# The second slice of a two-stage MoE kernel and its sweep, reordered as one list of single steps

## The chip, the cores and the metric

The kernel runs on one core of a Trainium2 chip. The metric is the device time of one execution in microseconds. The median of three runs of the kernel before is 983.5 us (981.6 to 984.88).

## The reference

Attention over eightfold mean-pooled keys and values feeds a gated MoE block, and that a second block:

```python
x = attention(q, mean_pool8(k), mean_pool8(v))      # 4 x 8 heads, 576 x 64
x = x.reshape(2304, 512)                            # tokens x d_model
xn = x / sqrt(mean(x * x) + 1e-6) * rms_g           # first block
g, val = xn @ w_gate, xn @ w_val                    # d_ff = 1536
x = (g * sigmoid(g) * val) @ w_out
return ((x @ w_a) * (x @ w_b)) @ w_out2             # second block
```

## The kernel before

Every fp32 product is made of three TensorE matmuls on a high and a low part of each operand (`wl*xh`, `wh*xh`, `wh*xl`). ACT makes the high part by a cast (`ah`, `sh`, `rh`, `bh`, `woh`, `hh`, `xh_t`), and DVE or GpSimd (POOL) the low part by a subtraction (`al`, `sl`, `rl`, `bl`, `wol`, `hl`, `xl_t`). Each of them needs both the fp32 source and the high part, and TensorE needs both parts.

The first block's 2304 tokens go as tiles of 512 and 256, and as two slices of 768. A slice is cut into halves of 384 columns, and gate and value for one block f of 128 of the 1536 hidden features (12 blocks) are made with seven half-products instead of eight. These are the tokens `N<f>.1` to `.7` of the second slice (six matmuls of 384 columns each), `N<f+1>.6` being a product of block f that is put off. The other tokens of a block:

- `p1`, `p5`, `u2`: ACT copies of PSUM banks (L1295); `d1` to `d3`: DVE adds another bank (L1299); `z1`, `z2`: SiLU on ACT (L1303); `d4`, `d5`: the products gate x value (L1307, L1312), and their stores to DRAM as `h`.
- `e1` to `e4`: sums of weights (`sf`, L1326 to L1332), on DVE, or on POOL with a "!"; `ca`, `cs`, `cr`, `cb`: casts of weights on ACT (L1349); `la`, `ls`, `lr`, `lb`: their lows (L1355), on POOL, or on DVE with a "!".

A sweep follows each slice. It multiplies `h` with `w_out` and adds up 12 blocks in six banks, the tokens `U<f>.0` to `.5` in the second sweep: three matmuls of 512 columns in `.0` to `.3`, six of 256 in `.4` and `.5`; 72 adds in all (L1429). `U<f>.f` fetches weights (`wo_again`) and `h` (`hf`, a part of 512 columns and one of 256) by three DMAs; `.w` and `.x` make `woh` (ACT, L1400) and `wol` (L1403: POOL, or DVE with "!"); `.h0`, `.h1`, `.k0`, `.k1` make `hh` (ACT, L1413) and `hl` of both parts (L1416: DVE, or POOL with "!"). `Ue0` to `Ue5` evict the banks (`ev`, ACT, or DVE with "!") and store them. The first slice and its sweep have the same tokens with M and Q for N and U.

Four engines (TensorE, ACT, DVE, POOL) issue in the order in which the tokens are called, a list of words written out by hand; DMA issues on SP are ordered by the scheduler. Buffers are few: the three tiles `p1` hold the snapshot `p1`, the evictions `ev` and the 512-column part of `hf` in turn, two tiles `u2` the snapshot `u2` and the other part of `hf`, and each weight operand but `b` has two.

Before, the second slice's tokens form a regular pattern, the same for each f. The second sweep's list has a "+" behind each of its 72 adds; at these, the steps of `second_front` are spread evenly: four loads, the opening of a pool, the conversion of four weight blocks of the second block from the input's 64-bit words (ACT twice, DVE twice, POOL once each: L610, L611, L622, L634, L641), the loads of its x, its x forms (casts L845, lows L850, differences L854), and the weight operands of its f = 0 and 1 (`combine`: L939, L946, L961 to L967).

Of the kernel before, what the change touches and what calls it, by code (L numbers as in the profile page):

```python
# [85 lines left out]
N3.e1 N3.e2 N2.2 N2.p5 N3.la N3.e4 N3.cs N2.3 N2.d1 N2.z1 N3.ls N3.e3 N2.4 N2.u2 N3.cr N2.5 N2.d2
N2.z2 N3.lr N2.6 N1.d5 N2.cb N2.7 N2.d3 N2.d4 N2.lb N3.1 N3.p1 N4.ca N4.e1 N4.e2 N3.2 N3.p5 N4.la
N4.e4 N4.cs N3.3 N3.d1 N3.z1 N4.ls N4.e3 N3.4 N3.u2 N4.cr N3.5 N3.d2 N3.z2 N4.lr N3.6 N2.d5 N3.cb
N3.7 N3.d3 N3.d4 N3.lb N4.1 N4.p1 N5.ca N5.e1 N5.e2 N4.2 N4.p5 N5.la N5.e4 N5.cs N4.3 N4.d1 N4.z1
N5.ls N5.e3 N4.4 N4.u2 N5.cr N4.5 N4.d2 N4.z2 N5.lr N4.6 N3.d5 N4.cb N4.7 N4.d3 N4.d4 N4.lb N5.1  # L90
N5.p1 N6.ca N6.e1 N6.e2 N5.2 N5.p5 N6.la N6.e4 N6.cs N5.3 N5.d1 N5.z1 N6.ls N6.e3 N5.4 N5.u2 N6.cr
N5.5 N5.d2 N5.z2 N6.lr N5.6 N4.d5 N5.cb N5.7 N5.d3 N5.d4 N5.lb N6.1 N6.p1 N7.ca N7.e1 N7.e2 N6.2
N6.p5 N7.la N7.e4 N7.cs N6.3 N6.d1 N6.z1 N7.ls N7.e3 N6.4 N6.u2 N7.cr N6.5 N6.d2 N6.z2 N7.lr N6.6
N5.d5 N6.cb N6.7 N6.d3 N6.d4 N6.lb N7.1 N7.p1 N8.ca N8.e1 N8.e2 N7.2 N7.p5 N8.la N8.e4 N8.cs N7.3
N7.d1 N7.z1 N8.ls N8.e3 N7.4 N7.u2 N8.cr N7.5 N7.d2 N7.z2 N8.lr N7.6 N6.d5 N7.cb N7.7 N7.d3 N7.d4
N7.lb N8.1 N8.p1 N9.ca N9.e1 N9.e2 N8.2 N8.p5 N9.la N9.e4 N9.cs N8.3 N8.d1 N8.z1 N9.ls N9.e3 N8.4
N8.u2 N9.cr N8.5 N8.d2 N8.z2 N9.lr N8.6 N7.d5 N8.cb N8.7 N8.d3 N8.d4 N8.lb N9.1 N9.p1 N10.ca N10.e1
N10.e2 N9.2 N9.p5 N10.la N10.e4 N10.cs N9.3 N9.d1 N9.z1 N10.ls N10.e3 N9.4 N9.u2 N10.cr N9.5 N9.d2
N9.z2 N10.lr N9.6 N8.d5 N9.cb N9.7 N9.d3 N9.d4 N9.lb N10.1 N10.p1 N11.ca N11.e1 N11.e2 N10.2 N10.p5
N11.la N11.e4 N11.cs N10.3 N10.d1 N10.z1 N11.ls N11.e3 N10.4 N10.u2 N11.cr N10.5 N10.d2 N10.z2  # L100
N11.lr N10.6 N9.d5 N10.cb N10.7 N10.d3 N10.d4 N10.lb N11.1 N11.p1 N11.2 N11.p5 N11.3 N11.d1 N11.z1
U0.f N11.4 N11.u2 N11.5 N11.d2 N11.z2 U0.w U0.x U0.h0 N11.6 N10.d5 N11.cb U0.k0 U0.h1 N11.7 N11.d3
N11.d4 N11.lb U0.k1 U1.f
""".split()
SECOND_END = """
U0.0 + U1.w U0.1 + N12.6 N11.d5 U2.f U1.x U1.h0 U0.2 + U1.k0 U1.h1 U0.3 + U1.k1 U0.4 + U0.5 + U1.0
+ U3.f U2.w U1.1 + U2.x U2.h0 U1.2 + U2.k0 U2.h1 U1.3 + U2.k1 U1.4 + U1.5 + U2.0 + U4.f U3.w U2.1 +
U3.x U3.h0 U2.2 + U3.k0 U3.h1 U2.3 + U3.k1 U2.4 + U2.5 + U3.0 + U5.f U4.w U3.1 + U4.x U4.h0 U3.2 +
U4.k0 U4.h1 U3.3 + U4.k1 U3.4 + U3.5 + U4.0 + U6.f U5.w U4.1 + U5.x U5.h0 U4.2 + U5.k0 U5.h1 U4.3 +
U5.k1 U4.4 + U4.5 + U5.0 + U7.f U6.w U5.1 + U6.x U6.h0 U5.2 + U6.k0 U6.h1 U5.3 + U6.k1 U5.4 + U5.5  # L110
+ U6.0 + U8.f U7.w U6.1 + U7.x U7.h0 U6.2 + U7.k0 U7.h1 U6.3 + U7.k1 U6.4 + U6.5 + U7.0 + U9.f U8.w
U7.1 + U8.x U8.h0 U7.2 + U8.k0 U8.h1 U7.3 + U8.k1 U7.4 + U7.5 + U8.0 + U10.f U9.w U8.1 + U9.x U9.h0
U8.2 + U9.k0 U9.h1 U8.3 + U9.k1 U8.4 + U8.5 + U9.0 + U11.f U10.w U9.1 + U10.x U10.h0 U9.2 + U10.k0
U10.h1 U9.3 + U10.k1 U9.4 + U9.5 + U10.0 + U11.w U10.1 + U11.x U11.h0 U10.2 + U11.k0 U11.h1 U10.3 +
# [1445 lines left out]
```

## Time and profile before

| what | value |
|---|---|
| runs | 981.6, 983.5, 984.88 us |
| profiled execution | 982.69 us, span 981.0 us |
| granted TensorE clock | 0.993 of full speed, over the span |
| TensorE busy | 948.0 us (97%) |
| DVE, ACT, POOL busy | 620.9, 476.1, 339.7 us |

The span is the time from the first to the last instruction of the profiled execution; its device time is 1.69 us longer. Busy shares are of the span. A wait is put down to the instruction whose semaphore came last.

### The profile page before, as it was taken

The numbers are of one execution on the slowest core, as the hardware profiler recorded it, in microseconds if no ns is written. First come the engines' busy times: TensorE is split into PE (matmuls) and PEld (weight loads), VectorE is DVE, ScalarE is ACT, GpSimd is POOL, SyncE is SP. The second block draws the span as 40 slices with busy tenths as digits, with TensorE's granted clock in tenths as the row PEclk, the third lists the DMA queues.
The fourth block names the chain that finished last, engine by engine and source line by source line (L and its number), as shares of the span: only waits on it lengthen the run. The fifth ranks groups of instructions, "written<-read, shape, count | busy, mean of one in ns | idle before, by whom it ended". The sixth has DMA issues, their size and how long they took to land.

```text
span 981.0 us, 14651 instructions
## 1 busy us (share of the span) xinstructions
PE 948.0 (97%) x5194; PEld 860.2 (88%) x5194; DVE 620.9 (63%) x1070; ACT 476.1 (49%) x914; POOL 339.7 (35%) x326
## 2 busy tenths in 40 slices
...
GB/s 305 192 229 241 194 86 122 137 126 98 33 60 49 65 186 146 149 61 53 65 228 150 153 130 122 150 127 132 132 138 150 132 113 218 182 161 97 151 106 65
DMA packets 67945, 133.34 MB, mean 136 GB/s; under 512 B 7457, under 2 KB 31265, under 8 KB 67873
## 3 DMA queue, kind: packets, MB, share of 16 engines
...
q8 instruction: 41, 0.67, 0.3%
...
## 4 chain that ended last, share of the span: by engine, by line
PE 82%; DVE 5%; DMA 4%; ACT 3%; issue 2%; POOL 2%; SPq 1%; DVEq 0%; ACTq 0%; POOLq 0%
PE X L1029 24%; PE o L1132 15%; PE Y L1029 12%; PE o L1429 6%; PE Z L1029 6%; PE acc L691 6%; PE v L683 4%; PE g L683 4%; PE av L476 3%; PE sc L406 1%; POOL wol L1403 1%; DMA hf<-h 1%; PE eP L453 1%; PE xP L512 1%; DMA q<-in_q_dram 1%
## 5 line engine op out<-in xcount | busy, mean ns | idle before, releaser
L1110 DVE TENSOR_TENSOR hl<-hf,hh 128x768 fp32r<-128x768 f32 x36 | 35.5, 991 | 93.4 <-ACT hh L1109 93.4
L1132 PE MATMUL o<-woh,hl 128*128 128x512 f32 x216 | 85.8, 397 | 0.0
L1132 PE MATMUL o<-woh,hh 128*128 128x512 f32 x216 | 85.0, 394 | 0.0
L1132 PE MATMUL o<-wol,hh 128*128 128x512 f32 x216 | 84.7, 392 | 0.0
L1429 PE MATMUL o<-hh,wol 128*128 128x256 f32 (+1 forms) x192 | 67.5, 351 | 10.6 <-POOL wol L1403 10.6
L1109 ACT CAST hh<-hf 128x768 fp32r<-128x768 f32 x36 | 29.8, 834 | 87.0 <-PE o L1132 79.3
L1429 PE MATMUL o<-hh,woh 128*128 128x256 f32 (+1 forms) x192 | 66.6, 347 | 0.0
L1429 PE MATMUL o<-hl,woh 128*128 128x256 f32 (+1 forms) x192 | 66.5, 346 | 0.0
L641 POOL TENSOR_TENSOR w<-w,st 128x512 int32<-128x512 int32 x20 | 26.2, 1308 | 110.9 <-DVE w L634 70.8
L1037 ACT COPY p<-X 128x384 f32<-128x384 f32 x36 | 17.2, 478 | 89.7 <-PE X L1029 86.7
L673 POOL TENSOR_TENSOR wl<-wf,wh 128x512 fp32r<-128x512 f32 x27 | 35.7, 1330 | 68.2 <-ACT wh L669 68.2
L1429 PEld LDWEIGHTS o<-hh,wol 128*128 128x128 f32 x192 | 37.6, 196 | 15.8 <-POOL wol L1403 11.6
L1132 PEld LDWEIGHTS o<-woh,hh 128*128 128x128 f32 x216 | 40.5, 188 | 10.1
L1132 PEld LDWEIGHTS o<-wol,hh 128*128 128x128 f32 x216 | 40.6, 188 | 9.5
L1132 PEld LDWEIGHTS o<-woh,hl 128*128 128x128 f32 x216 | 40.6, 188 | 9.3
L611 ACT ACTIVATE st<-st 128x512 int32<-128x512 uint32 x72 | 48.0, 667 | 0.0
L1416 DVE TENSOR_TENSOR hl<-hf,hh 128x512 fp32r<-128x512 f32 (+1 forms) x37 | 30.3, 837 | 25.9 <-ACT hh L1413 25.9
L1029 PE MATMUL X<-xh_t,rl 128*128 128x384 f32 x120 | 41.0, 342 | 4.6 <-ACT u L1295 3.9
L641 POOL TENSOR_TENSOR wo<-wo,st 128x512 int32<-128x512 int32 x16 | 21.8, 1365 | 66.6 <-ACT p L1037 28.9
L691 PE MATMUL acc<-ht,wo 128*128 128x512 f32 (+1 forms) x112 | 43.5, 531 | 0.0
L1429 PEld LDWEIGHTS o<-hl,woh 128*128 128x128 f32 x192 | 37.4, 195 | 4.9 <-DVE hl L1416 0.6
L1029 PE MATMUL Y<-xh_b,rl 128*128 128x384 f32 x120 | 41.5, 346 | 0.2 <-ACT p L1037 0.2
(228 smaller groups left out, 3129.4 us busy)
## 6 DMA issues: line engine op xcount, KB each, us to landing
...
h<-p SPq DMA_DIRECT2D x60, 192.0 KB, 1.9
h<-u SPq DMA_DIRECT2D x60, 192.0 KB, 1.9
wo_again<-wd SPq DMA_DIRECT2D x36, 256.0 KB, 2.7
...
wd<-wo SPq DMA_DIRECT2D x24, 256.0 KB, 2.1
```

The lines of the kernel that those rows point to most:

```text
L476: nc.tensor.matmul(view[:, h0:h0 + len(hs), :D + 1], lhs, VB[b % 2][:, c, j0:j0 + len(hs), :], start=((c, bk) in ((0, 0), (2, 1))), stop=( ...
L611: nc.scalar.activation(out=low, in_=low.bitcast(U32), func=AF.Copy, scale=2.0 ** -29)
L641: (nc.vector if boot["alt"] else nc.gpsimd).tensor_tensor(out=bits, in0=bits, in1=low, op=ALU.add)
L673: (nc.vector if boot["alt"] else nc.gpsimd).tensor_sub(wl, wf[ph, f, i], wh.bitcast(F32))
L683: nc.tensor.matmul(bank[:, :n], w[:, c, :], x[:, c, cols], start=(c == 0 and i == 0), stop=(c == KD - 1 and i == 2),)
L691: nc.tensor.matmul(accs[c][:, cols], w[:, c, :], ht[:, :cols.stop - cols.start], start=(f == 0 and cols.start == 0), stop=(f == NF - 1),)
L1029: nc.tensor.matmul(dst[:, :HALF], w[:, c0 + c, :], x[:, c, :], start=(start and i == 0), stop=(stop and i == 5), skip_group_check=True,)
L1109: nc.scalar.copy(hh, hf)
L1110: nc.vector.tensor_sub(hl, hf, hh.bitcast(F32))
L1132: nc.tensor.matmul(accs[i], x[:, sub], y, start=(f == 0 and j == 0), stop=(f == NF - 1 and j == 2),)
L1416: (nc.gpsimd if boot["alt"] else nc.vector).tensor_sub(lo, src, hi.bitcast(F32))
L1429: nc.tensor.matmul(dst, w[:, c, :], x, start=(f == 0 and j == 0 and at == 0), stop=(f == NF - 1 and j == 2), skip_group_check=True,)
```

## The change

The second slice, its sweep and the second block's first operands are now one list. `second_front` no longer returns steps that are spread over the sweep; it registers a name for each: `Zo` (the pool), `ZL0`, `ZL1` (loads of x), `Z<form>c`, `Z<form>l` (cast and low of an x form), `Zd0` to `Zd3` (differences), `x0.0` to `x3.3` (four steps for each weight block's conversion), and `Z0.`, `Z1.` with `e1` to `e4`, `c` and `l` (weight operands). For each of them a "!" now chooses the engine. In the list, blocks x0 and x1 are converted wholly during the slice, x2 and x3 by half. The order within the slice and the sweep is no longer a repeated pattern, and many steps change engine: of the slice's 48 weight sums 30 are on POOL (4 before), of its 36 lows `la`, `ls`, `lr` 28 are on DVE (6 before), of the sweep's 12 `wol` nine are on DVE (none before), and of the 24 `hl` seven are on POOL (none before). The end of the first sweep is rewritten too. Matmuls and their operands are the same.

```diff
-N0.3 Jt3l Qe5 N0.p5 N1.e4 N0.4 N0.u2 N1.e3! N0.7 N1.cr Jt4l N1.lr! N0.d3 N0.5 N0.d1 N0.z1 N0.d2
-N0.z2 N0.d4 N1.1 N1.p1 N2.ca N2.e1 N2.e2 N1.2 N1.p5 N2.la N2.e4 N2.cs N1.3 N1.d1 N1.z1 N2.ls N2.e3
...
+Qe0 N1.e2 Jt4c N0.lr! Qe1 Qe2 Q11.5 Q11.4 Jt3l N0.1 N1.e3! Qe3! N0.p1 l Jt4l N0.2 N0.4 N1.ca N1.cs
+N0.u2 N0.3 N0.p5 Qe4! Qe5! N1.la! N1.e4! N1.ls N0.7 N0.5 N2.ca N2.e1 N1.1 N0.d3 N1.6 N2.e2 N1.3
...
+N10.z1 N10.cb N10.7 N9.z2 N11.1 N10.d2 N10.z2 x1.3 N10.lb N10.d3 N11.6 N11.cr N11.p1 N10.d4 N9.d4
+N11.cb N11.2 N11.4 N11.p5 N11.u2 N11.lr! x3.1 N11.lb! N10.d5 N11.5 U0.f N11.7 N11.d2 U0.h1 N11.d3
...
-U11.k1 U10.4 + U10.5 + U11.0 Ue0 + U11.1 Ue1! + U11.2 Ue2 + U11.3 Ue3! + U11.4 Ue4 + U11.5 Ue5! +
...
+Z1.la! Zb10l U10.3 Zt2l Zt3l Zb11l Ue2 U11.3 U10.5 Z1.cr Z1.ls! U10.4 U11.k1 Z1.lr Ue3 U11.4 Zd3!
+Ue4! U11.5 Z1.lb! Zt4c Ue5! Zt4l
...
-        def pairs(steps, n):
-            out = [steps[i::n] for i in range(n)]
-            out, i = [], 0
-            for j in range(n):
-                k = -(-(len(steps) - i) // (n - j))
-                group_, i = steps[i:i + k], i + k
-                out.append(lambda g=group_: [st() for st in g])
-            return out
-
-        loads, steps = load_and_build(0, new, quarter)
-        first_ = pairs(convert(0, 0) + convert(0, 1) + combine(0), 8)
-        first_[3] = lambda st=first_[3]: (st(), loads[0]())
-        first_[7] = lambda st=first_[7]: (st(), loads[1]())
-        rest = convert(1, 0) + convert(1, 1) + combine(1)
-        return [load_part] * 4 + [open_pool] + first_ + pairs(steps + rest, 24)
+        part = {}
+        loads = load_x(0, quarter, part)
...
+
+        def cast(i):
+            hi, lo = XC[(1, 0), i] = new(0, i)
+            for c in range(2):
+                nc.scalar.copy(hi[:, c], part[FORM_OF[i]][c])
+
+        def low(i):
+            hi, lo = XC[(1, 0), i]
+            eng = nc.gpsimd if boot["alt"] else nc.vector
+            for c in range(2):
+                eng.tensor_sub(lo[:, c], part[FORM_OF[i]][c], hi[:, c].bitcast(F32))
+
+        def less(i):
+            dst, a, b = LESS[i]
+            eng = nc.gpsimd if boot["alt"] else nc.vector
+            for c in range(2):
+                eng.tensor_sub(part[dst][c], part[a][c], part[b][c])
...
+        names["Zo"] = open_pool
+        names["ZL0"], names["ZL1"] = loads
+        for i in FORM_OF:
+            names[f"Z{i}c"] = lambda i=i: cast(i)
+            names[f"Z{i}l"] = lambda i=i: low(i)
+        for i in range(4):
+            names[f"Zd{i}"] = lambda i=i: less(i)
+
+        def conversion(n):
+            box, (begin, sign, merge, end) = convert_steps(new_wf2)
+
+            def last():
+                end()
+                load_part()
+
+            for i, st in enumerate((begin, sign, merge, last)):
+                names[f"x{n}.{i}"] = st
+
+        for n in range(4):
+            conversion(n)
...
+        def sums(f, i):
+            if (f, i // 3) not in box:
+                box[f, i // 3] = wf_p.tile([P, KD, P], F32, tag="wf", name=f"sf_{f}_{i}")
+            t, s0 = box[f, i // 3], box.get((f, 0))
+            eng = nc.gpsimd if boot["alt"] else nc.vector
+            if i == 1:
+                eng.tensor_add(t[:, 0:2], w(f, 1, 0), w(f, 1, 1))
+            elif i == 2:
+                eng.tensor_sub(t[:, 2:4], t[:, 0:2], w(f, 0, 0))
+            elif i == 3:
+                eng.tensor_sub(t[:, 2:4], w(f, 0, 1), s0[:, 2:4])
+            else:
+                eng.tensor_sub(t[:, 0:2], w(f, 0, 0), w(f, 1, 0))
...
+        def part_cast(f, key):
+            src = source(f, key)
+            n = src.shape[1]
+            hi, lo = box[f, key] = [
+                two["e"].tile([P, n, P], F32R, tag=f"{key}{e}{f}", name=f"{key}{e}_1_{f}", bufs=1)
+                for e in "hl"
+            ]
+            nc.scalar.copy(hi, src)
+            for i, nm in enumerate({"a": (A00, A01), "s": (S1, S2), "r": (S3, S4), "b": (A11,)}[key]):
+                WC[(1, None, f), nm] = (hi, lo, 2 * i)
+
+        def part_low(f, key):
+            hi, lo = box[f, key]
+            (nc.vector if boot["alt"] else nc.gpsimd).tensor_sub(lo, source(f, key), hi.bitcast(F32))
+
+        for f in range(2):
+            for i in range(1, 5):
+                names[f"Z{f}.e{i}"] = lambda f=f, i=i: sums(f, i)
+            for key in "asrb":
+                names[f"Z{f}.c{key}"] = lambda f=f, key=key: part_cast(f, key)
+                names[f"Z{f}.l{key}"] = lambda f=f, key=key: part_low(f, key)
...
+        second_front()
         for t in SECOND:
             token(t)
-        side = second_front()
-        total = SECOND_END.count("+")
-        at = done = 0
-        for t in SECOND_END:
-            if t != "+":
-                token(t)
-                continue
-            at += 1
-            want = -(-len(side) * at // total)
-            while done < want:
-                side[done]()
-                done += 1
```

The start of the slice on ACT. `p_0` and `u_0` are the snapshots of block 0, `ev<-o_4` the eviction of the first sweep's bank 4, `rh`, `ah`, `sh` casts of weights, and `xh_t` the cast of an x form. Before:

```order
419 L1349 CAST ah_4223<-wf_0_1_313 128x512
420 L1295 COPY p_0_2_4226<-X_2_4216 128x384
421 L884 CAST xh_t_2_4228<-x_0_1_3208 128x768
422 L248 COPY ev<-o_4_3562 128x512
423 L248 COPY ev<-o_5_3661 128x512
424 L1295 COPY p_0_2_4256<-Y_2_4236 128x384
425 L1295 COPY u_0_2_4266<-X_2_4216 128x384
```

After the change:

```order
417 L249 COPY ev<-o_0_3635 128x512
418 L885 CAST xh_t_2_4191<-x_0_1_3208 128x768
419 L249 COPY ev<-o_1_3614 128x512
420 L249 COPY ev<-o_2_3585 128x512
421 L1368 COPY p_0_2_4226<-X_2_4214 128x384
422 L1422 CAST ah_4244<-wf_0_1_313 128x512
423 L1422 CAST sh_4247<-sf_4172 128x512
424 L1368 COPY u_0_2_4250<-X_2_4214 128x384
425 L1368 COPY p_0_2_4259<-Y_2_4231 128x384
```

The evictions of `o_4` and `o_5` (and `o_3`) have left ACT; those of `o_0` to `o_2` stand ahead of both snapshots, and two casts of weights between `p` and `u` where the second `xh_t` and two evictions stood.

The middle of the sweep. `wol_7` and its like are lows of the sweep's weights, `wf` conversion ends, `al_…`, `sl_0`, `rl` and `bl` lows of the second block's weights. POOL before:

```order
223 L641 TENSOR_TENSOR wf_1_0_5314<-wf_1_0_5314,st_0_0_5217 128x512
224 L641 TENSOR_TENSOR wf_1_0_5335<-wf_1_0_5335,st_0_1_5226 128x512
225 L1403 TENSOR_TENSOR wol_3_5348<-wo_again_5280,woh_3_5347 128x512
226 L946 TENSOR_TENSOR al_5373<-wf_1_0_5314,ah_5372 128x512
227 L946 TENSOR_TENSOR sl_5404<-sf_0_5375,sh_5403 128x512
228 L946 TENSOR_TENSOR rl_5408<-sf_0_5379,rh_5407 128x512
229 L1403 TENSOR_TENSOR wol_4_5420<-wo_again_5341,woh_4_5419 128x512
230 L946 TENSOR_TENSOR bl_5441<-wf_1_0_5335,bh_5440 128x256
231 L1403 TENSOR_TENSOR wol_5_5479<-wo_again_5413,woh_5_5478 128x512
232 L1403 TENSOR_TENSOR wol_6_5533<-wo_again_5472,woh_6_5532 128x512
233 L1403 TENSOR_TENSOR wol_7_5597<-wo_again_5526,woh_7_5596 128x512
```

DVE before, while POOL is at `wol_7`; `xl_b`, `xl_t` are lows of x forms, `x<-x,x` differences:

```order
655 L1416 TENSOR_TENSOR hl_6_5553<-hf_6_5476,hh_6_5552 128x256
656 L854 TENSOR_TENSOR x_0_0_0_5382<-x_1_1_0_5463,x_0_0_0_5382 128x384
657 L854 TENSOR_TENSOR x_0_0_1_5383<-x_1_1_1_5464,x_0_0_1_5383 128x384
658 L850 TENSOR_TENSOR xl_b_0_5559<-x_1_1_0_5463,xh_b_0_5558 128x384
659 L850 TENSOR_TENSOR xl_b_0_5559<-x_1_1_1_5464,xh_b_0_5558 128x384
660 L854 TENSOR_TENSOR x_1_0_0_5457<-x_1_1_0_5463,x_1_0_0_5457 128x384
661 L854 TENSOR_TENSOR x_1_0_1_5458<-x_1_1_1_5464,x_1_0_1_5458 128x384
662 L850 TENSOR_TENSOR xl_t_0_5585<-x_0_0_0_5382,xh_t_0_5584 128x384
663 L850 TENSOR_TENSOR xl_t_0_5585<-x_0_0_1_5383,xh_t_0_5584 128x384
664 L1416 TENSOR_TENSOR hl_7_5604<-hf_7_5528,hh_7_5603 128x512
```

DVE after the change, around the same `wol_7`; `sf` are weight sums of the second block, `hl_7` hidden lows:

```order
655 L1489 TENSOR_TENSOR hl_7_5575<-hf_7_5545,hh_7_5574 128x256
656 L1055 TENSOR_TENSOR sf_1_5606<-wf_1_1_4856 128x256
657 L1057 TENSOR_TENSOR sf_1_5606<-sf_1_5606,wf_1_1_4559 128x256
658 L1476 TENSOR_TENSOR wol_7_5584<-wo_again_5541,woh_7_5583 128x512
659 L1059 TENSOR_TENSOR sf_4_5475<-wf_1_0_4407,sf_1_5237 128x256
660 L1489 TENSOR_TENSOR hl_7_5595<-hf_7_5543,hh_7_5594 128x512
661 L1015 TENSOR_TENSOR xl_t_0_5565<-x_0_0_0_4901,xh_t_0_5564 128x384
662 L1015 TENSOR_TENSOR xl_t_0_5565<-x_0_0_1_4902,xh_t_0_5564 128x384
663 L1061 TENSOR_TENSOR sf_4_5658<-wf_1_1_4559,wf_1_1_4856 128x256
664 L1476 TENSOR_TENSOR wol_8_5651<-wo_again_5587,woh_8_5650 128x512
```

`wol_7` has moved from POOL's queue to DVE's, between two hidden lows; the run of differences and lows of x beside it is down to one form's low ahead of the next `wol`.

The end of the sweep on DVE. `hl_11` is the last hidden low of the sweep, in two parts, `ev` an eviction. Before:

```order
680 L1416 TENSOR_TENSOR hl_10_5759<-hf_10_5697,hh_10_5758 128x512
681 L1416 TENSOR_TENSOR hl_10_5769<-hf_10_5699,hh_10_5768 128x256
682 L961 TENSOR_TENSOR sf_1_5784<-wf_1_1_5731 128x256
683 L962 TENSOR_TENSOR sf_1_5784<-sf_1_5784,wf_1_1_5681 128x256
684 L966 TENSOR_TENSOR sf_1_5797<-wf_1_1_5681,sf_1_5784 128x256
685 L967 TENSOR_TENSOR sf_1_5797<-wf_1_1_5681,wf_1_1_5731 128x256
686 L1416 TENSOR_TENSOR hl_11_5808<-hf_11_5747,hh_11_5807 128x512
687 L1416 TENSOR_TENSOR hl_11_5818<-hf_11_5749,hh_11_5817 128x256
688 L246 COPY ev<-o_1_5222 128x512
```

After the change, first the run's head and then its tail; the rows between are lows of x forms:

```order
673 L1489 TENSOR_TENSOR hl_11_5780<-hf_11_5754,hh_11_5779 128x512
674 L1476 TENSOR_TENSOR wol_11_5787<-wo_again_5752,woh_11_5786 128x512
675 L1082 TENSOR_TENSOR rl_0_5687<-sf_4_5475,rh_0_5686 128x512
676 L1489 TENSOR_TENSOR hl_10_5773<-hf_10_5648,hh_10_5772 128x256
677 L1082 TENSOR_TENSOR sl_0_5707<-sf_1_5237,sh_0_5706 128x512
678 L1082 TENSOR_TENSOR al_1_5656<-wf_1_1_4559,ah_1_5655 128x512
679 L1015 TENSOR_TENSOR xl_b_0_5616<-x_0_1_0_4905,xh_b_0_5615 128x384
```

```order
685 L1015 TENSOR_TENSOR xl_b_0_5518<-x_1_1_0_5095,xh_b_0_5517 128x384
686 L1015 TENSOR_TENSOR xl_b_0_5518<-x_1_1_1_5096,xh_b_0_5517 128x384
687 L1082 TENSOR_TENSOR sl_1_5736<-sf_1_5606,sh_1_5735 128x512
688 L1489 TENSOR_TENSOR hl_11_5809<-hf_11_5756,hh_11_5808 128x256
689 L247 COPY ev<-o_4_5286 128x512
690 L1082 TENSOR_TENSOR bl_1_5799<-wf_1_1_4856,bh_1_5798 128x256
```

The weight sums have gone elsewhere. Weight lows `rl_0`, `sl_0`, `al_1`, `sl_1` and eight lows of x forms (`xl_b`, `xl_t`) now stand between `wol_11` and the last `hl_11`.

## Rows read from the trace of the kernel before

**Rows 1.** The page, part 1: busy time and share of the span, by engine.

```profile
PE 948.0 (97%) x5194; PEld 860.2 (88%) x5194; DVE 620.9 (63%) x1070; ACT 476.1 (49%) x914; POOL 339.7 (35%) x326
```

**Rows 2.** TensorE's waits, 398 to 558 us: total, times, longest.

```profile
PE o L1429 <- POOL wol L1403: 10.6, 4, 5.9
PE X L1029 <- ACT u L1295: 3.0, 1, 3.0
```

**Rows 3.** TensorE's timeline, its pauses in 404 to 541: start, length, what, idle before.

```profile
405.96 0.44 PE L1029 MATMUL X<-xh_t,rl 128*128 128x384 f32 x1 [2.96 <-ACT u L1295]
...
491.06 0.50 PE L1429 MATMUL o<-hh,wol 128*128 128x512 f32 x1 [1.04 <-POOL wol L1403]
...
508.25 0.50 PE L1429 MATMUL o<-hh,wol 128*128 128x512 f32 x1 [2.81 <-POOL wol L1403]
...
515.17 0.50 PE L1429 MATMUL o<-hh,wol 128*128 128x512 f32 x1 [0.88 <-POOL wol L1403]
...
533.88 0.80 PE L1429 MATMUL o<-hh,wol 128*128 128x512 f32 x1 [5.91 <-POOL wol L1403]
```

**Rows 4.** Windows of 5 us: busy by engine, PEclk granted clock, DMA share, GB/s.

```profile
510.00:515.00 5.00, 4.29 (x19) 3.41 (x18) 3.61 (x5) 3.46 (x8) 4.35 (x3) 0.73 0.84 252
515.00:520.00 5.00, 4.83 (x27) 4.25 (x28) 4.02 (x8) 2.77 (x7) 2.25 (x3) 1.00 0.62 187
535.00:540.00 5.00, 5.00 (x15) 4.03 (x14) 0.00 (x0) 0.00 (x0) 0.51 (x1) 0.50 0.00 0
```

**Rows 5.** The chain that ended last: start, length, what.

```profile
370.23 25.07 PE o L1429 x141
...
415.10 3.13 PE X L1029 x18
...
480.66 3.13 PE X L1029 x18
...
495.92 0.36 SPq L1089
...
526.01 7.82 POOL wol L1403
```

**Rows 6.** Windows by stretch: first slice, first sweep, four stretches of second slice and sweep.

```profile
239.17:342.48 103.31, 102.36 (x629) 101.27 (x629) 76.46 (x142) 68.49 (x136) 52.32 (x62) 1.00 0.16 55
350.68:395.30 44.62, 44.62 (x260) 39.22 (x260) 27.83 (x48) 22.58 (x44) 11.43 (x11) 1.00 0.51 153
398.66:415.10 16.44, 13.48 (x69) 13.16 (x68) 10.54 (x17) 8.38 (x18) 3.97 (x3) 0.90 0.53 177
415.10:480.66 65.56, 65.56 (x380) 65.56 (x379) 46.70 (x81) 39.34 (x82) 41.72 (x36) 1.00 0.16 57
491.06:533.88 42.82, 33.21 (x174) 28.05 (x174) 33.08 (x53) 22.57 (x48) 25.52 (x15) 0.95 0.67 208
533.88:557.70 23.82, 23.82 (x121) 20.69 (x122) 13.79 (x15) 8.62 (x17) 14.54 (x10) 0.87 0.26 86
```

**Rows 7.** DMA issues, 398 to 560: count, KB, median us to landing.

```profile
h<-u SPq DMA_DIRECT2D x12, 192.0 KB, 1.9
x<-ev SPq DMA_DIRECT2D x6, 256.0 KB, 2.5
hf<-h SPq DMA_DIRECT2D x12, 128.0 KB, 2.6
```

**Rows 8.** Groups by line and shape, 398 to 558: busy us, mean ns, idle before.

```profile
L1330 DVE TENSOR_TENSOR sf<-wf,sf 128x256 f32<-128x256 f32 x10 | 14.0, 1402 | 0.0
L1416 DVE TENSOR_TENSOR hl<-hf,hh 128x512 fp32r<-128x512 f32 x12 | 12.1, 1011 | 14.8 <-ACT hh L1413 14.8
L1328 DVE TENSOR_TENSOR sf<-sf,wf 128x256 f32<-128x256 f32 x11 | 4.7, 424 | 0.3
L1299 DVE TENSOR_TENSOR u<-u,Y 128x384 f32<-128x384 f32 x12 | 6.6, 554 | 4.5 <-PE Y L1029 2.4 <-issue 2.1
...
L1355 DVE TENSOR_TENSOR rl<-sf,rh 128x512 fp32r<-128x512 f32 x2 | 1.4, 686 | 3.1 <-ACT rh L1349 3.1
...
L1355 POOL TENSOR_TENSOR rl<-sf,rh 128x512 fp32r<-128x512 f32 x10 | 13.0, 1295 | 10.3 <-ACT rh L1349 9.2 <-issue 1.1
...
L1413 ACT CAST hh<-hf 128x512 fp32r<-128x512 f32 x12 | 7.4, 616 | 4.5 <-DMA hf<-h 4.5
```

More of the change, by code (lines that the diff above doesn't have):

```diff
@@ L86 @@
[L86 to L114, printed above, removed]
-U11.k1 U10.4 + U10.5 + U11.0 Ue0 + U11.1 Ue1! + U11.2 Ue2 + U11.3 Ue3! + U11.4 Ue4 + U11.5 Ue5! +
+Jb10c Q4.2 Q4.0 Q5.w Q5.k1! S17.9 Q4.3 Q6.h1 Q6.k1 Q5.k0! Q5.x! N0.e2! Q5.0 S16.11 S16.12 N0.e4
@@ new lines @@
+S17.10 Q5.5 N0.cb Q5.3 Q6.w Q5.2 Jb00l Q6.h0 Jb10l Q6.x! Q7.f Q5.4 N0.e3! Q6.4 Q6.5 Q6.k0 S17.11
+Q7.h1 Q5.1 Q8.f Q6.1 Q6.2 Q7.k1! S17.12 N0.lb Q9.f Q7.w Jb11c Jd0 Q7.x! Q6.3 Q6.0 Jd2 Q7.5 Q7.4
+Q7.h0 Q7.k0 Q8.h0 Jt1c Q7.3 Q8.w Q7.1 Q8.k0 Q8.x! Q8.h1 Q8.k1 Q7.2 Q9.h1 Q7.0 Q8.4 Q8.5 Jt1l Q9.k1
+Q9.w Q9.h0 Q8.3 Q8.0 Jd1 Q10.f Q9.x! Q8.1 Q8.2 Q11.f Jt2c Q9.k0 Q10.h1 Q10.h0 Q9.5 Q10.k1 Q9.2 Q9.0
+Jd3 Q10.w Q10.k0! Q9.4 Q9.3 Q9.1 Q10.x! Q10.2 Q11.h0 Jt2l Q10.3 Jb11l Q10.0 Q11.k0! Q11.h1 Q11.w
+Q11.x! Q10.1 N0.cs Q10.4 Q11.k1 Q10.5 Q11.1 N0.ca N0.ls! Q11.0 N1.e1! Q11.3 Jt3c N0.cr N0.la! Q11.2
```

46 lines of the change are left out of this document (37 added, 9 removed).

## The prediction

> **What bounds the kernel now.** I read the page first: TensorE (PE) is busy 948.0 of 981.0 us [rows 1]. All but 33 us is matmuls, and the change adds and removes none, so only PE's idle and slow time can move. Next I took PE's waits for the stretch that the diff rewrites, from the second slice's first matmul (398.66) to the second stage's first (557.70): 3.0 us behind ACT, once, and 10.6 us behind GpSimd's (POOL's) `wol`, four times [rows 2]. The timeline places them: 2.96 at the start of the slice, 1.04 where the sweep begins, and 2.81, 0.88 and 5.91 inside the sweep [rows 3], 13.6 us in all.
>
> Idle time is not the whole loss. In 5-us windows the granted clock is 0.73 after the stall of 2.81 and 0.50, the lower level of 1.2 GHz, after that of 5.91, but 1.00 after that of 0.88 [rows 4]. So I compare the stretch with the same work undisturbed. In the chain, one output block f of the slice repeats every (480.66 - 415.10)/9 = 7.284 us [rows 5]; 12 make 87.4. The sweep has 288 matmuls in 72 adds; in the first sweep 141 of the same mixture take 25.07 us [rows 5], so 288 take 51.2, or 0.71 an add. The floor is 138.6 us, the stretch takes 557.70 - 398.66 = 159.04 (its ends are the edges of the first and last of four windows [rows 6]), and **20.4 us** are to be had: 13.6 idle and 6.8 mostly half clock, some 2.3 for each of the three long stalls.
>
> The table by stretch shows where nothing is lost: PE is busy throughout in 415.10 to 480.66, and in the first sweep [rows 6]. That first sweep and the first slice (102.36 of 103.31) are already written in the irregular step-by-step style that the second now gets. The regular stretch 491.06 to 533.88 is busy 33.21 of 42.82 [rows 6].
>
> **The change part by part.** *Start of the slice, -2.96 and its clock.* Before, ACT has the evictions `ev` of `o_4` and `o_5` ahead of the two snapshots `p` and `u` that free PE's banks. An eviction needs one of three tiles, freed only when an earlier one's store lands, 2.5 us after issue [rows 7]. Now `o_3` to `o_5` go to DVE and no eviction stands between `p` and `u`. What is late next: the first snapshot's own tile is that of `o_1`. After the last add to `o_1` come five adds and two products ahead of the one that needs the snapshot, 5 x 0.71 + 2 x 1.04 = 5.6 us. ACT can evict `o_0` only one add later: 0.7, `ev` 0.62 (priced as ACT's cast of 512 columns, `hh`), a cast `xh_t` of 768 columns 0.93 (by size), `ev` of `o_1` 0.62 [rows 8], then 0.36 to issue [rows 5], 2.5 to land, and the snapshot 0.55 (as DVE on 384 columns): 6.3. The sum has whole steps rounded up; **left: 0.6** (0 to 2.96).
>
> *Start of the sweep, -1.04.* The first `wol` moves from POOL to DVE (0.69 for 1.30, the prices of `rl` on each [rows 8]). It now stands behind this chain from the end of product N10.7: three DVE operations of 0.55 (N10.d3, N10.d4, N9.d4), N9's store 1.9, issue 0.36, the 128-KB load 2.6 [rows 5, 7], cast U0.h1 at most 0.62, on ACT behind it N11.z2 0.55, on DVE N11.d4 and N11.d1 1.1, `wol` 0.69: 9.5 us [rows 8]. Eight products cover 8 x 1.04 = 8.3. **Left: 1.0** (0 to 2), the cast being of half the columns.
>
> *Inside the sweep, -9.60 and the clock.* The four waits have one cause, POOL. `wol_3` stands behind two conversion ends, `wol_4` behind `al`, `sl` and `rl`, and `wol_7` starts at 526.01 and takes 7.82 us [rows 5] where its like takes 1.30. During it DVE runs one subtraction after another, each reading two SBUF operands. The same collision shows in the slice: the one of four equal sums that shares its time with a POOL low, L1330, takes 1402 ns, its neighbour L1328 424 [rows 8]. Now nine of twelve `wol` are on DVE, all but f = 3, 6 and 10; two of the four weight blocks are converted wholly in the slice and two halfway; and only one of eight second-stage weight lows stays on POOL. I take all three stalls as gone.
>
> Here the Trainium skill (SBUF — State Buffer, "SBUF: two separate sides") speaks against a clean gain: the shared DVE/GpSimd port pair "is an exclusive lock, not a bandwidth split", and a DVE operation with two SBUF inputs takes part in it against a GpSimd operation that reads SBUF. The trace agrees, with 7.82 for 1.30 and 1402 for 424. By that rule moving work between the two engines gains only what DVE is quicker by, and leftover POOL lows can still be starved; that is the first rival, and its sum is there.
>
> *End of the sweep, a new wait.* Four form lows of the second stage and four weight lows now stand on DVE between `wol_10` and the last hidden low `hl_11`, where before two sums and the hidden low stood. The weight tile of f = 11 is free when U9.5 ends. From there: cast 0.62, `wol_11` 0.69, `rl` 0.69, `hl_10` 0.42, `sl` 0.69, `al` 0.69, eight form lows of 0.55, `sl_1` 0.69, `hl_11` 0.42 [rows 8]: 9.3. U11.4 comes after ten adds, 7.1. **Left: 2.0**, a little less since `hl` can run while the cast waits; it lies above the 0.88 that cost no clock and below the 2.81 that did, so I add none (0 to 2.2, plus 2.3 if the clock falls).
>
> *In the slice, 0.* POOL takes 30 of the 48 sums, DVE 28 of the 36 larger weight lows, and the conversions add a dozen operations. ACT is busy 39.34 and POOL 41.72 of 65.56 us there [rows 6], so there is room, and weights are made one block or more ahead: the shortest lead I find in the order is N2's `bl` before N3.6, some 3.3 us. Cover gone, each late low costs its lateness; that is the second rival. *Start of the second stage, 0:* the same operands are needed by the same products; I leave ±1.
>
> Sum against the profiled execution: 982.69 - 20.4 + 0.6 + 1.0 + 2.0 = 965.9. The median of the runs is 983.5, 0.8 above, so **966.7 us**.
>
> **The rivals.** *1. The pair binds the sweep (0.20).* Priced by rows 8, what DVE and POOL do there with two SBUF operands is: `wol` 9 x 0.69 + 3 x 1.30, hidden lows 10 x 0.69 + 2 x 1.30 of 512 columns and 7 x 0.42 + 5 x 0.65 of 256, weight lows 5 x 0.69 + 2 x 0.42 + 1.30, form lows 12 x 0.55, eight sums 5 x 0.42 + 3 x 0.65, differences 4 x 0.55 + 4 x 0.98, conversion steps some 3: 51 us, beside 51 of matmuls (POOL at 1.30 for 512 columns, less by size). In the undisturbed slice before, it is four lows (3 x 1.30 + 0.65), four sums (1.7) and one product (0.55), 6.8 of 7.28, and PE never waits: 93% is bearable, 100% may not be. If the excess comes out at PE, and `rl_1` and a pair of differences on POOL (1.30 and 1.96) fall into the last DVE run, the wait there grows by up to 3.3 and draws the clock, 2.3: with some 2 more for the rest 966.7 + 2 to 8, so 969 to 975, middle 971.5. For it: `hl` in the sweep before has a mean of 1011 ns, not 686 [rows 8]. Against: part of that work is needed only after the sweep ends. (By the lock of the Trainium skill, SBUF — State Buffer, quoted above, none of it overlaps.)
>
> *2. Slower: starved lows in the slice (0.07).* DVE now has long stretches of two-operand work in the slice too. A POOL low as starved as `wol_7` ends 7.8 - 1.3 = 6.5 late; with 3.3 of lead PE stands 3.2, and with the clock 5.5 are lost. Three leave nothing worth the name (16.8 - 16.5); from four on the kernel is slower, one in every three blocks giving 966.7 + 22 = 988.7. Against it: in the slice DVE's runs are cut by operations that wait for a product.
>
> *3. No change: loads bind the sweep (0.04).* A sweep needs 12 x 640 KB, 7.7 MB in 51 us, 150 GB/s, with three and two buffers for the hidden tiles. Had loads been what was late, removing `wol` would uncover them: 66 us of sweep again and 983 in all. Against it: the first sweep moves 153 GB/s with PE never idle [rows 6]; a 128-KB load lands in 2.6 [rows 7], and two buffers last for two blocks, 8.5.
>
> **How the numbers follow.** The forecast, 963 to 970, has 0.63; the rest, 0.06, is a full gain with the second stage's start better too, 961 to 963. Below 961 there is nothing left to take but matmuls. The range for 8 in 10 is 961 to 975: it takes in rival 1's bulk. This kernel's measurement tells some 0.3% (3 us) from no change. Faster: 0.63 + 0.06 + 0.20 = 0.89 less a little for rival 1 with worse, 0.88; same 0.05; slower 0.07.
>
> **What would show it.** Right: PE busy about 102 of each 103 us from the slice's start to the second stage's; no wait of PE behind POOL `wol` but for f = 3, 6 and 10, if any; three small waits, at N0.4, U0.4 and U11.4, of which the last is the largest; granted clock 1.00 but perhaps there; second stage starting near 541 instead of 557.70. Rival 1 shows as several waits spread over the sweep behind `hl` or `wol`, and `hl` means near 1 us; rival 2 as POOL lows of several us before 480 and PE waits behind L1428; rival 3 as ACT casts waiting for `hf` or `wo_again`. The prediction is wrong if an operation that before was early is now last in its queue: a store or load behind the `ZL` loads on SP, which this order leaves to the scheduler, is the one I can price least.

## The result and the profile after

The changed kernel takes 970.14 us (median of 4 runs, 967.97 to 972.82) against 984.12 (4 runs). The ratio is 0.9864, with a 95% interval of 0.9833 to 0.9895: 14 us faster. The forecast was 966.7, its range 961 to 975. The profiled execution took 970.12 us, 12.6 less than that of before; the sum had 16.8.

TensorE's waits in the rewritten stretch, 395 to 560 us (total, times, longest), answer to [rows 2]:

```profile
PE X L1102 <- ACT p L1368: 2.9, 1, 2.9
PE o L1502 <- DVE wol L1476: 1.8, 1, 1.8
PE X L1102 <- ACT p L1110: 1.3, 1, 1.3
PE o L1502 <- DVE hl L1489: 1.1, 1, 1.1
PE X L1102 <- ACT u L1110: 0.3, 1, 0.3
```

The timeline of TensorE places them (start, length, what, idle before); it answers to [rows 3]:

```profile
403.83 0.69 PE L1102 MATMUL X<-xh_t,sl 128*128 128x384 f32 x1 [2.92 <-ACT p L1368]
...
492.53 0.38 PE L1502 MATMUL o<-hh,wol 128*128 128x256 f32 x1 [1.79 <-DVE wol L1476]
...
542.89 0.39 PE L1502 MATMUL o<-hl,woh 128*128 128x256 f32 x1 [1.13 <-DVE hl L1489]
...
555.00 0.45 PE L1102 MATMUL X<-xh_t,sl 128*128 128x384 f32 x1 [1.29 <-ACT p L1110]
```

No wait is behind POOL any more. The first three are the three that the prediction named, at N0.4, U0.4 and U11.4; the fourth is in the second stage. By stretch (columns as in [rows 6]: start of the slice, rest of the slice, sweep):

```profile
398.65:410.47 11.82, 8.90 (x45) 8.58 (x43) 6.53 (x10) 3.97 (x9) 2.25 (x4) 0.86 0.61 201
410.47:490.58 80.11, 80.11 (x463) 79.89 (x462) 56.49 (x103) 48.99 (x106) 37.21 (x42) 1.00 0.29 93
492.53:541.60 49.07, 49.07 (x278) 43.13 (x278) 33.78 (x55) 27.69 (x57) 17.77 (x14) 1.00 0.53 164
```

TensorE is busy throughout the slice behind its start, and throughout the sweep but for its two ends. The clock is below 1.00 in the first stretch alone.

Executions differ by a few us ahead of the slice, where nothing is changed. So below I compare the stretch by itself, in each profiled execution, from the starts of three matmuls in TensorE's timeline: the slice's first, the sweep's first and the second stage's first.

| kernel | slice's first at | slice | sweep | both |
|---|---|---|---|---|
| before | 398.66 | 92.40 | 66.64 | 159.04 |
| changed | 398.65 | 93.88 | 51.65 | 145.53 |
| e1 | 400.02 | 90.59 | 60.35 | 150.94 |
| e2 | 398.24 | 92.13 | 57.70 | 149.83 |
| e3 | 396.80 | 94.08 | 52.92 | 147.00 |
| e4 | 397.57 | 89.40 | 51.65 | 141.05 |
| e5 | 397.61 | 93.58 | 51.70 | 145.28 |
| e6 | 399.10 | 93.75 | 51.19 | 144.94 |
| e7 | 398.53 | 93.28 | 55.18 | 148.46 |
| e8 | 397.88 | 94.07 | 59.72 | 153.79 |
| e9 | 399.53 | 93.98 | 53.21 | 147.19 |
| e10 | 400.13 | 88.06 | 50.58 | 138.64 |
| e11 | 396.57 | 88.06 | 50.60 | 138.66 |
| e12 | 399.58 | 92.49 | 60.50 | 152.99 |

The gain is in the sweep: 15.0 us. The slice has lost 1.5. Product N12.6 (1.04 us) counts in the sweep in before, e1, e2 and e12, and in the slice in all the others; for the same matmuls the sweep has gained 13.9 and the slice lost 0.4. The second stage has lost 0.9 (424.22 us behind its first matmul, 423.30 before).

Each row is one execution. Before, e1, e2 and e12 run nearly the same slice, and it takes 90.59 to 92.49 us: in e1 the granted clock stays at 1.00 after a wait of 2.73, in the other three it falls after waits of 2.76 to 3.07. So a difference of less than 2 us between two rows may be the clock alone.

### The profile page after: what moved, and what is told of

It is laid out like the page before. It is cut to its first block, busy times and chain, and to the rows that moved or that the text cites. A ratio compares the mean times of both kernels' runs of the same rounds, so it can differ in the third digit from the quotient of the medians.

```text
span 968.4 us, 14619 instructions
## 1 busy us (share of the span) xinstructions
PE 942.2 (97%) x5194; PEld 856.8 (88%) x5194; DVE 614.7 (63%) x1073; ACT 475.1 (49%) x915; POOL 315.1 (33%) x322
## 5 line engine op out<-in xcount | busy, mean ns | idle before, releaser
L1502 PE MATMUL o<-hh,wol 128*128 128x512 f32 (+1 forms) x192 | 65.4, 340 | 1.8 <-DVE wol L1476 1.8
L1502 PE MATMUL o<-hl,woh 128*128 128x512 f32 (+1 forms) x192 | 64.7, 337 | 1.1 <-DVE hl L1489 1.1
L1502 PE MATMUL o<-hh,woh 128*128 128x512 f32 (+1 forms) x192 | 64.9, 338 | 0.0
L1102 PE MATMUL X<-xh_t,sl 128*128 128x384 f32 x120 | 41.4, 345 | 4.6 <-ACT p L1368 2.9
L684 PE MATMUL g<-xh,wl 128*128 128x256 f32 (+1 forms) x104 | 39.1, 376 | 2.6 <-ACT ht L783 2.3
```

The costliest lines, as they stand in the source:

```text
L684: nc.tensor.matmul(bank[:, :n], w[:, c, :], x[:, c, cols], start=(c == 0 and i == 0), stop=(c == KD - 1 and i == 2),)
L1102: nc.tensor.matmul(dst[:, :HALF], w[:, c0 + c, :], x[:, c, :], start=(start and i == 0), stop=(stop and i == 5), skip_group_check=True,)
L1502: nc.tensor.matmul(dst, w[:, c, :], x, start=(f == 0 and j == 0 and at == 0), stop=(f == NF - 1 and j == 2), skip_group_check=True,)
```

## The experiments

**e1, one low moved.** In the kernel before, only the weight low of f = 7 goes to DVE.

```diff
-U6.0 + U8.f U7.w U6.1 + U7.x U7.h0 U6.2
+U6.0 + U8.f U7.w U6.1 + U7.x! U7.h0 U6.2
```

> The kernel before with one step changed: the weight low of f = 7 in the second sweep goes from POOL to DVE. Theory (POOL is shut out by DVE's two-operand run, and nothing else is late for f = 7): the 5.91 us stall at the first add of f = 7 shrinks to under 1 and the half clock after it goes, so 6 to 8 us less than before, 976 to 978. Rival (the operand is late for a reason of its own, or stands as long in DVE's queue): the stall stays, now behind DVE, and the time stays at 984.

976.36 us, ratio 0.9937 (0.9913 to 0.9960). The stall of 5.91 is gone and the sweep is 6.3 us shorter. Instead there is one of 0.50 behind DVE's `hl` of f = 7, and one of 1.58 at the next low on POOL, f = 8. Nearly all of the stall was the low itself; what else is late for f = 7 costs 0.50.

**e2, nine lows moved.** In the kernel before, "!" on U.x for all f but 3, 6 and 10.

> The kernel before with nine of the twelve weight lows of the second sweep on DVE, as in the changed kernel (all but f = 3, 6, 10), and nothing else. Theory (the wait behind POOL's low is nearly all that the sweep lost): the stalls of 1.04, 5.91 and most of 2.81 and 0.88 go, 10 to 14 us less, 970 to 974; the 2.96 at the start of the slice stays. Rival (DVE, which still has the conversions and the forms, becomes the bound): new waits of TensorE behind DVE's lows of 3 us or more in all, 976 to 984.

974.99 us, ratio 0.9921 (0.9894 to 0.9948): between theory and rival. The sweep is 8.9 us shorter, where the whole change gains 13.9 on the same matmuls. What is left is 2.22 behind the low of f = 3, which stays on POOL behind two conversion ends, and six smaller waits, 0.20 to 0.97, all behind DVE. So DVE with the old order becomes late too, though not by as much as the rival had it.

**e3, all lows back on POOL.** The changed kernel without the nine "!".

> The changed kernel with all twelve weight lows of the second sweep on POOL again. Theory (engine of the low decides): waits behind POOL's low come back, 5 to 15 us in all, 976 to 986. Rival (the conversions in the slice and the new order are what helped, POOL now being free of them): no more than 1 us of new waits, 970 to 972.

971.1 us, ratio 0.9884 (0.9861 to 0.9906); it overlaps the changed kernel's. The theory fell: with all twelve on POOL, none waits. POOL's `wol` in that kernel, 480 to 558 us (its count, shortest, median and longest in ns):

```profile
L1476 POOL TENSOR_TENSOR wol<-wo_again,woh x12: 1270/1302/1748, 489.6 to 535.3; 128x512 fp32r<-128x512 f32 x12
```

The longest takes 1.75 us, not 7.82. The sweep is 1.3 us longer than the changed kernel's, but not by a low on POOL: its first add waits 1.94 behind a product (DVE `p`, L1385), 1.79 behind `wol` in the changed kernel, and behind that wait the clock falls here and not there. The window 490 to 495 us (columns as in [rows 6]), first in e3, then in the changed kernel:

```profile
490.00:495.00 5.00, 4.12 (x17) 3.74 (x18) 3.94 (x5) 2.55 (x6) 4.41 (x4) 0.66 0.76 230
490.00:495.00 5.00, 3.21 (x22) 2.72 (x20) 4.35 (x7) 4.04 (x10) 2.12 (x3) 1.00 0.65 181
```

The engine of the low, which I had named first, is a remedy in the old order and in the new one is worth nothing that these runs can tell.

**e7 and e8, the two other parts.** In e7, five conversion steps and a sum go from the slice back to the sweep's first blocks; in e8, behind the changed slice, the sweep has the old regular order and engines.

```diff
-U0.4 U0.5 U0.k0 Zo U1.h0 U0.0 U0.3 U0.1 Zb00c x3.2 U1.k1! U1.k0! U1.x! U0.2 U2.w U1.4 U1.5 Zb00l
+U0.4 x0.2 x1.1 U0.5 U0.k0 Zo U1.h0 U0.0 U0.3 x0.3 x1.2 U0.1 Zb00c x3.2 U1.k1! U1.k0! U1.x! U0.2
+U2.w U1.4 x1.3 U1.5 Zb00l
```

> The changed kernel with the last steps of the conversion of two weight blocks (x0.2, x0.3, x1.1 to x1.3) and the weight sum behind them moved from the slice to the first blocks of the sweep, POOL doing both ends there. If the room made by the conversions in the slice is a large part of the gain: waits of 2 us or more in the first three blocks of the sweep, 973 to 978. If the spread of the steps over the sweep is what counts: under 1 us of new waits, 970 to 972.

> The changed kernel's slice, with two blocks converted in it, and behind it the sweep in the old regular order with the old engines, the steps of the second stage spread evenly as before. If the conversions are what counts: 970 to 973. If the order of the sweep counts: the second wait of before (behind the three second-stage weight lows on POOL) and the one in the run of x forms come back, 4 to 10 us with their clock, 974 to 982.

975.39 us (0.9921, 0.9898 to 0.9944) and 977.27 (0.9939, 0.9920 to 0.9958). Both count: the sweep is 3.5 us longer with the conversions back (new waits of 1.03 behind `hl` of f = 0 and 1.97 behind `wol` of f = 1, on DVE), and 8.1 longer in the old order. Of the 8.1 some 1.7 is slow clock behind the first add's wait of 1.81 (0.72 granted in 490 to 495 us, 0.94 in 495 to 500), which the old order need not have caused. The rest of the 13.9, 5.9, is what e8's slice brings to the old order (66.64 less N12.6's 1.04, less 59.72). In e8 the waits of early blocks don't return, but the one in the run of x forms does, 4.27, on the same low:

```profile
520.75 8.98 POOL L1475 TENSOR_TENSOR wol<-wo_again,woh 128x512 fp32r<-128x512 f32 x2 [3.43 <-ACT woh L1472]
```

The first of these two takes 7.75 us.

**e5, e6 and e9, a run made on purpose.** In the changed kernel eleven of DVE's operations were drawn together beside the low of f = 8; in e5 that low is on POOL, in e6 on DVE, in e9 on POOL with two ACT casts exchanged.

```diff
-U6.3 U6.2 U7.0 U9.f U8.k1! U7.5 U10.f U8.w Zt1l Z1.ca Z1.e4 U8.x! U7.2 U8.h0 U7.3 U7.1 U7.4 U8.k0!
+U6.3 U6.2 U7.0 U9.f U8.k1! U7.5 U10.f U8.h0 U8.k0 U8.w Z1.ca U8.x U7.2
+Zt1l Zb10l Zb11l Zd2 Z0.e3 Z1.e4 Z0.la! U7.3 U7.1 U7.4
```

> The changed kernel with eleven of DVE's two-operand operations of the second half of the sweep (lows of three x forms, a difference, two weight sums, a weight low) drawn together into one run beside the weight low of f = 8, which stands on POOL. Theory (POOL's low can't proceed while DVE runs two-operand work back to back): that low lasts 4 to 7 us where its like took 1.29, TensorE waits 2 to 4 us behind it, with a clock loss, 973 to 976. Rival (a low on POOL costs 1.3 whatever DVE does; before, something else held it): no wait of more than 0.5, 969 to 971.

> The same run of eleven, with the weight low of f = 8 on DVE ahead of it; the only difference to the kernel before this one. Theory: no wait behind it, the time is that of the changed kernel, 969 to 971. Rival (the run itself, which delays DVE's later lows by some 6 us, is what costs): waits of 2 us or more behind DVE's lows of f = 9, 973 to 976.

> The kernel with the run of eleven and the weight low of f = 8 on POOL, with two ACT casts exchanged, so that the low becomes ready some 0.6 us later, when DVE's run has begun; it was ready 0.04 us before the run in the kernel without the exchange, and held its 1.30 us while DVE's first low waited. Theory (whoever has begun keeps the port, and DVE's run keeps it as long as it is without a gap): POOL's low now lasts 5 to 7 us, TensorE waits 2 to 5 us behind it, 973 to 978. Rival (POOL gets in between two DVE operations, and before it was something else): the low lasts under 2.5 us, 970 to 972.

971.2 (0.9873, 0.9851 to 0.9895), 969.76 (0.9861, 0.9843 to 0.9878) and 972.29 us (0.9893, 0.9871 to 0.9915): none tells from the changed kernel, and in e5 and e9 the theory missed: TensorE does not wait behind POOL. Each of the three has one wait inside the sweep instead, 1.14, 0.63 and 1.12 us behind DVE's low of f = 9, which the run delays (the rival of e6, at less than its 2 us). In e5 POOL's low was ready at 521.79, just ahead of the run; it took 1.30 and DVE's first low stood. In e9 it was ready at 526.13, within the run, and got in all the same. DVE in e9, then POOL:

```profile
525.66 1.02 DVE L1015 TENSOR_TENSOR xl_t<-x,xh_t 128x384 fp32r<-128x384 f32 x2
526.60 3.05 DVE L1015 TENSOR_TENSOR xl_b<-x,xh_b 128x384 fp32r<-128x384 f32 x4
```

```profile
526.13 1.69 POOL L1476 TENSOR_TENSOR wol<-wo_again,woh 128x512 fp32r<-128x512 f32 x1 [3.10 <-ACT woh L1473]
```

Four `xl_b` take 1.95 us in e5 and 3.05 here: the first stood while POOL had its turn. So a run of two-operand work does not by its length alone keep POOL out.

**e12, a break in the run.** In the kernel before, one DVE write of two words ahead of the low t2.

```diff
 def low(i, h, k):
     hi, lo = XC[key, i]
+    if key == (1, 0) and i == "t2":
+        nc.vector.memset(lo.bitcast(F32)[:, 0, :2], 0.0)
```

> The kernel before with one DVE instruction added: two words written into a tile of the x forms ahead of the low t2, in the middle of the run during which POOL's weight low of f = 7 stood for 7.82 us; its result is overwritten by that low. In the run of eleven POOL did get in after 0.4 us, so what keeps it out is open. Theory (POOL gets in where DVE's run has an instruction that reads nothing from SBUF, as it did at the shift that ended the long wait): the low ends about 1.5 us after the added write, the stall of 5.91 falls below 1.5 and the time by 4 to 8 us, 975 to 979. Rival (such an instruction opens nothing; the end of DVE's run decides): the low still takes 6 us or more, 982 to 984.

976.74 us, ratio 0.9953 (0.9934 to 0.9972). DVE's timeline in this kernel:

```profile
526.47 1.02 DVE L856 TENSOR_TENSOR x<-x,x 128x384 f32<-128x384 f32 x2
527.44 0.06 DVE L850 MEMSET xl_t<- 128x2 f32 x1
527.62 1.92 DVE L852 TENSOR_TENSOR xl_t<-x,xh_t 128x384 fp32r<-128x384 f32 x2
```

and POOL's:

```profile
526.76 1.89 POOL L1405 TENSOR_TENSOR wol<-wo_again,woh 128x512 fp32r<-128x512 f32 x1 [3.90 <-ACT woh L1402]
532.55 4.83 POOL L1405 TENSOR_TENSOR wol<-wo_again,woh 128x512 fp32r<-128x512 f32 x2 [3.91 <-ACT woh L1402]
```

A write of 0.06 us turns 7.82 [rows 5] into 1.89: the low ends at 528.65, 1.2 behind the write, and DVE's next low takes 1.45 of the 1.92. The sweep is 6.1 us shorter. The next `wol`, ready at 532.55, again waits for the shift L622 that ended the run before. The shift reads one tile, so the expectation's "reads nothing" does not fit it; what the write and the shift share is that neither reads two. The low behind the write also waits for it (0.12 us of gap), so whether the kind of the instruction or the gap lets POOL in is not told apart. What is left for f = 7 and 8 is as in e1: 0.76 behind `hl`, 1.56 behind POOL's `wol`, and a sweep of 60.50 us beside 60.35.

**e4, the late load.** In the changed kernel POOL writes two words into the tiles of the weight loads of f = 1, so that the two that stood among the last stores of the first sweep, 512 KB each, can't be issued there.

```diff
+        if ph == 1 and f == 1:
+            nc.gpsimd.memset(t.bitcast(F32)[:, :2], 0.0)
         if i < 2:
             nc.sync.dma_start(out=t, in_=w[f])
```

> The changed kernel with two 512-KB weight loads of the second stage (f = 1) held back by two words that POOL writes into their tiles, so that they no longer stand among the first sweep's last stores. Theory (the store whose tile the first snapshot needs took 4.6 us because a load ran beside it): it lands in about 2.5, TensorE's wait of 2.92 at the start of the slice falls to 0.5 to 1 and the clock does not fall, 2 to 3.5 us less than the changed kernel, 966.5 to 968. Rival (the stores only slow each other): the wait stays at 2.5 to 3, 970.

965.36 us, ratio 0.9826 (0.9806 to 0.9847): better than the theory had it. SP's issues in the changed kernel:

```profile
397.06 0.33 SPq L1512 DMA_DIRECT2D x<-ev  x1
398.17 0.33 SPq L590 DMA_DIRECT2D st<-in_moe_w_a_dram  x1
398.60 1.62 SPq L1512 DMA_DIRECT2D x<-ev  x3
400.76 0.34 SPq L590 DMA_DIRECT2D st<-in_moe_w_b_dram  x1
```

DMA, 394 to 406 us there (count, KB, median us to landing):

```profile
x<-ev SPq DMA_DIRECT2D x4, 256.0 KB, 4.6
```

and 394 to 404 in e4:

```profile
x<-ev SPq DMA_DIRECT2D x4, 256.0 KB, 2.0
```

The snapshot comes at 399.31 instead of 403.30, TensorE does not wait at the start of the slice at all, and the slice is 4.5 us shorter: 2.92, the half clock, and 0.26 less of the wait at its end.

**e10 and e11, the rest.** On top of e4, steps moved at both ends of the sweep (e10), and in the second stage's first group one side step less (e11).

```diff
-U0.f N11.7 N11.d2 U0.h1 N11.d3 Z0.e1! N11.z2 N11.d4 N11.3 N11.d1 U0.k1! U0.h0 U0.w N11.z1 U0.x! N12.6
+U0.f U0.w N11.7 N11.d2 N11.z2 U0.h1 N11.d3 U0.x! Z0.e1! N11.d4 N11.3 N11.d1 U0.k1! U0.h0 N11.z1 N12.6
-Zt2l Zt3l Zb11l Ue2 U11.3 U10.5 Z1.cr Z1.ls! U10.4 U11.k1 Z1.lr
+Zt2l Zt3l U11.k1 Zb11l Ue2 U11.3 U10.5 Z1.cr Z1.ls! U10.4 Z1.lr
-        group(0, 0, loads + idle + steps[:4])
-        group(1, 0, steps[4:])
+        group(0, 0, loads + idle * 2 + steps[:3])
+        group(1, 0, steps[3:])
```

> The changed kernel with the two loads held back, and with steps moved: at the slice's end the cast and the low of the first sweep weights and the SiLU of block 11 ahead of the cast that waits for a load, and at the sweep's end the last hidden low ahead of one form low and one weight low. Theory: the waits of 1.53 and 1.13 us go to under 0.4 each, 2 to 2.5 us less than with the loads alone, 962.5 to 963.5. Rival (the load of the hidden tile, not the order on ACT and DVE, is late at the start of the sweep): 1 us or more stays there, 964 to 965.

> The same with the second stage's first group taking one of its side steps less, so that ACT's casts that wait for late loads of x stand behind the next snapshot. Theory (the wait of 1.04 at the second stage's start is a snapshot queued behind such a cast): it goes, 0.5 to 1 us less than without, 962 to 963. Rival: the wait only moves to a later product, no difference.

964.4 us (0.9818, 0.9797 to 0.9839) and 963.41 (0.9800, 0.9780 to 0.9821): the best two, though their intervals overlap with that of e4. By its time e10 falls to the rival (964 to 965); by its waits the theory holds, 0.19 and none, and the stretch is 2.4 us shorter than in e4, while that execution took longer outside the stretch. TensorE's waits in e10, 395 to 562 us:

```profile
PE X L1104 <- ACT p L1112: 1.2, 2, 1.0
PE X L1104 <- ACT u L1112: 0.3, 1, 0.3
PE o L1504 <- DVE p L1374: 0.2, 1, 0.2
```

Of the waits in the stretch 0.2 is left, and it takes 138.64 us; the floor of the prediction was 138.6. For the second stage's start e11 tells nothing. It was made for e4's wait of 1.04, which comes after 54 matmuls of the stage; in e10 that one is gone and one of 1.00 comes after 18, and in e11 0.99 stands there still, behind the same snapshot.

## Why the prediction was right, and where it was off

- **The floor and the sum of losses.** Right: e10 and e11 reach 138.64 and 138.66.
- **The number.** 970.14 lies just past the forecast's 963 to 970 and inside the range only by what was allowed for rival 1 (969 to 975), whose mechanism did not show. So the range held in part by luck; the sums below say where the 3 to 4 us went.
- **Inside the sweep, -9.60 and the clock.** Right in size: no wait is left there. Wrong in the step "nine of twelve `wol` are on DVE", which the prediction named first of three and did not tell apart from the others: in the new order the engine brings nothing that can be told (e3), though in the old one it brings 8.9 (e2). The last conversion steps done in the slice are worth 3.5 (e7) and the sweep's order with its engines up to 8.1 (e8). These overlap and don't add up. The cause behind the long wait stands: POOL's low shut out during DVE's run (e1, e8, e12). Why some runs shut it out and that of e9 does not stays open.
- **Start of the slice.** The term failed in size: 0.6 forecast, 2.92 measured, and 1.1 of slow clock (145.53 less 138.6 is 6.9, of it 5.84 idle). The chain was the right one, the snapshot's tile being that of `o_1`. But I priced its store at 2.5 us; it shared the DMA with a load that SP issued 0.43 us ahead of it, and landing took 4.6 (e4). The 2.5 is a median over stores with and without such a load [rows 7], and the trace of the kernel before had the price: its wait of 2.96 stood behind an eviction that began 0.07 us after a store had landed, a store that SP issued 0.6 us behind a weight load. SP there, then the DMA from 400 to 401 us:

```profile
399.55 0.33 SPq L589 DMA_DIRECT2D st<-in_moe_w_b_dram  x1
400.15 0.32 SPq L1439 DMA_DIRECT2D x<-ev  x1
```

```profile
x<-ev SPq DMA_DIRECT2D x1, 256.0 KB, 4.3
```

  The three stores ahead of that load landed in 2.0. So the change left the cause of this wait in place. The prediction had named a store behind the `ZL` loads on SP as what it could price least; the load was one of weights. It also took the last of its three waits for the largest; this one is.
- **Start of the sweep.** 1.0 forecast, 1.79 measured. The SiLU z2 stood on ACT behind a cast that waited 2.68 us for its load; e10, which takes it and the weights' cast and low out from behind it, leaves 0.19.
- **End of the sweep.** 2.0 forecast, 1.13 measured. DVE's run from `wol_11` to the last `hl` took 7.5 us (535.32 to 542.84), where the sum has 8.7: operations in a row overlap, so that four form lows took 1.96 and not 4 x 0.55:

```profile
535.32 0.69 DVE L1476 TENSOR_TENSOR wol<-wo_again,woh 128x512 fp32r<-128x512 f32 x1 [0.71 <-ACT woh L1473]
...
539.00 1.96 DVE L1015 TENSOR_TENSOR xl_t<-x,xh_t 128x384 fp32r<-128x384 f32 x4
...
542.42 0.42 DVE L1489 TENSOR_TENSOR hl<-hf,hh 128x256 fp32r<-128x256 f32 x1
```

  POOL's `rl_1`, which rival 1 had holding DVE up, was itself shut out, for 4.03 us:

```profile
539.95 4.03 POOL L1082 TENSOR_TENSOR rl<-sf,rh 128x512 fp32r<-128x512 f32 x1 [7.43 <-ACT rh L1076]
```

- **Start of the second stage.** 0 forecast within 1, 0.9 lost. SP issues all eight loads of x behind the last evictions' stores, from 546.71, 2.5 us after the stage's first matmul; before, two of them went out 0.9 ahead of it. But that is not shown to be the cause, nor the loss to be one: in e1, e2 and e12 two loads go out as early, and TensorE waits 0.69 to 0.82 at the place where it waits 0.35 before and 1.29 in the changed kernel (0.42 to 1.04 in e3 to e9). The second stage takes 423.3 to 424.0 us in before, e1, e2 and e12, and 423.6 to 424.4 in the changed kernel and e3 to e9.
- **The rivals.** The pair did not bind the sweep (49.07 of 49.07 busy; DVE's `hl` of 512 columns have a mean of 799 ns, not 1011 [rows 8]):

```profile
L1489 DVE TENSOR_TENSOR hl<-hf,hh 128x512 fp32r<-128x512 f32 x10 | 8.0, 799 | 7.5 <-ACT hh L1486 7.5
```

  No low starved TensorE in the slice (80.11 of 80.11), and loads bind nothing in a sweep of 51.65 us; one of them was late at its start, as said above.

The errors add up: +2.3 and +1.1 at the slice's start, +0.8, -0.9, +0.9, together 4.2, which is 16.8 less 12.6. The last 0.9 is no more than executions differ by there.
